# Filler products of ones, a second buffer for the first-stage result and fewer column products in an adaLN, state-space and routed-FFN kernel

## The chip, the cores and the metric

The kernel runs on one core of one Trainium2 chip, in one launch. A core has engines with a queue of instructions each: TensorE (PE in the profile, its weight loads PEld), VectorE (DVE), ScalarE (ACT), GpSimd (POOL) and SyncE (SP, which here only issues transfers). The metric is the device time of one execution in microseconds; before the change three runs took 553.38, 555.62 and 557.21 us, median 555.62.

## The reference, cut to what matters

One sequence of 2048 tokens of width 576 goes through two modulated layers. The shifts, scales and gates are six rows of a product of a condition vector with a 576 x 3456 matrix.

```python
mod = (_silu(c) @ w_mod).reshape(c.shape[0], 6, 1, -1)
sa, ca, ga, sb, cb, gb = (mod[:, i] for i in range(6))
x = A_u
h = _layernorm(x) * (1 + ca) + sa
x = x + ga * _A_ref(h, ...)          # long convolution over the sequence
h = _layernorm(x) * (1 + cb) + sb
x = x + gb * _B_ref(h, ...)          # 8 routed tokens through a SwiGLU FFN
...
def _A_ref(u, ...):                  # D = 576 channels, N = 128 poles, L = 2048
    P = jnp.exp((A * dt[:, None])[:, :, None] * pos[None, None, :])
    K = 2.0 * jnp.einsum("dn,dnl->dl", C, P).real
    y = irfft(rfft(u_t, 2 * L) * rfft(K, 2 * L), 2 * L)[:, :, :L]
    return y + u * D_skip
...
def _B_ref(x, ...):                  # x stays, 8 tokens get an update
    r = x @ w_r
    idx = jnp.argsort(-r, axis=-1)[:, :8]
    y = (_silu(x_sel @ w_gate) * (x_sel @ w_up)) @ w_down   # 576 -> 4608 -> 576
    return x + scatter(y * sigmoid(r_sel))
```

## The kernel before

**Stages.** The long convolution is done as a Fourier transform of length 4096, split in two steps. In the *front* the kernel loads parameters and tokens, makes the modulation rows (`mod_row`, L617 to L650), the layer norm's statistics (`ln_stats`, L681) and the first step of the transform of the tokens (`stage1`, L725): for each of 8 blocks `b` of two token columns, `ln_norm` makes normalised rows `hb` (L720), and four groups of products (L739 for the rows, L742 for the shift) go to two PSUM banks, from where ScalarE or VectorE copies them (L748) to tiles `xs0` and `xs1`. Four transfers of each block (L754) store them to the DRAM tensor `dX`. In the *middle* the convolution reads `dX` back (L912), transforms it (L923), transforms the taps (L937), multiplies, and goes back (L971). The taps come from 36 blocks of poles: magnitudes (L792, L798), sines and cosines (L809 to L832), products (L837 to L858), and a first transform step (L879); some of these blocks are made in the front beside the first stage. In the *tail* the router picks 8 tokens, the FFN weights come in (L1052), and the output is made and stored (L1242 to L1252).

**The order.** Nothing is ordered by a scheduler at run time: `Plan` holds every operation with the engines it may run on, an estimated cost, what it reads and writes, its ring of buffers, and its PSUM banks. `schedule` (L129) puts them in order by a list schedule over those estimates, with priorities from the longest chain to the end, to which seeded noise is added (`SEEDS`, L42); `emit` then writes each engine's queue in the order of planned starts. The planned times are estimates; what runs is the order. Changed costs, buffers or seeds so give a new order for the whole program.

**Rings.** `ring(name, key, bufs)` says that the operations on block `i` of a ring wait in the plan for those on block `i - bufs`; the tile pool gives the tile the same number of buffers. `xs0` and `xs1` have one each: the copies of block `b` wait until the stores of block `b - 1` have ended.

**Fillers.** `spare` (L207) looks at the planned gaps between TensorE's operations. Where a gap holds them, it sets `n` filler products ahead of the later operation, so many that the window of `WINDOW` = 3.4 us before that operation is planned busy to the share `SHARE`, each counted as `UNIT` = 0.27 us. None is set before planned time `FROM` = 12, nor while the bank `b5` is in use by others (from planned time `HOLD` = 130 on, until its last use). `idle` (L433) writes them: a 128 x 128 product of the identity with itself into `b5`, whose result nobody reads.

```python
n = min(int((t1 - t0 - self.GAP) / self.UNIT), math.ceil((self.SHARE * self.WINDOW - full) / self.UNIT))
if n > 0 and (t1 < self.HOLD or t0 > late) and t0 > self.FROM:
```

The identity is part of `csm`, which comes by a transfer (L444). `ones` is a 128 x 1 column that VectorE sets at the start (L429).

**The columns.** Late in the front `cols` (L1394) turns two modulation rows (`cb`, `sb`) into columns, with products of a piece of the row, 64 elements long, with a single one: 2 rows x 5 columns x 2 halves = 20 products (L1401).

A float32 product appears in the trace as two records, a bfloat16 or float16 product as one.

Of the kernel before, what the change touches and what calls it, by code (L numbers as in the profile page):

```python
# [11 lines left out]
F32 = mybir.dt.float32  # L12
# [9 lines left out]
L, D, NS, F = 2048, 576, 128, 4608  # L22
# [15 lines left out]
class Plan:  # L38

    LAT = {"V": .12, "A": .17, "P": .12, "T": .21, "Q": 0.0, "X": 0.0}  # L40
    LOOK, TABLE, RATE, FLY, AHEAD = .3, 1.28, 370.0, 2.0, 2.0
    SEEDS = ((15, 0.32), (789, 1), (1215, 0.32), (1311, 0.32), (1887, 0.32), (3271, 0.32), (4311, 0.32), (5223, 0.32), (5319, 0.32), (13159, 0.32), (16055, 0.32), (23663, 0.32), (35487, 0.32), (35511, 0.32), (36455, 0.32), (37575, 0.32), (39311, 0.32), (43039, 0.32), (62487, 0.32), (94159, 0.32), (220535, 0.32), (314815, 0.32), (322255, 0.32), (349359, 0.32), (362815, 0.32))  # L42
    wide = False
    BANKS, NARROW, HOLD = ("b0", "b1", "b2", "b3", "b4", "b5"), ("b5",), 130.0

# [4 lines left out]
    def ring(self, name, key, bufs):  # L50
        r = self.rings.setdefault(name, [])
        if key not in r:
            r.append(key)
            self.bufs[name, key] = bufs
        return (name, key)
# [73 lines left out]
    def schedule(self):  # L129
        self.link()  # L130
        for s, a in self.SEEDS:
            for o in self.ops:
# [74 lines left out]
    def spare(self):  # L207

        ts = [o for o in self.done if o.on == "T"]
        out, load = {}, []  # L210
        late = max((o.gone for o in self.done if o.need and set(o.names) & set(self.NARROW)), default=0.0)
        for a, b in zip(ts, ts[1:]):
            t0 = a.start + (a.cost["T"] if isinstance(a.cost, dict) else a.cost)
            t1 = b.start
            load.append((a.start, t0))
            while load and load[0][1] < t1 - self.WINDOW:
                load.pop(0)
            full = sum(y - max(x, t1 - self.WINDOW) for x, y in load)
            n = min(int((t1 - t0 - self.GAP) / self.UNIT), math.ceil((self.SHARE * self.WINDOW - full) / self.UNIT))
            if n > 0 and (t1 < self.HOLD or t0 > late) and t0 > self.FROM:  # L220
                out[b] = n
                load.append((t0, t0 + n * self.UNIT))
        return out

    GAP, WINDOW, UNIT, FROM, SHARE, idle = .3, 3.4, .27, 12.0, .8, None

    def emit(self):
        Plan.last = self
# [112 lines left out]
def adaln_s4d_mod_kernel(ctx, tc, u, par0, par1, head, wm, wr, wg, wu, wd, cs, cfg, cmv, out):  # L341
    nc = tc.nc
    V, S, P, T, Q = nc.vector, nc.scalar, nc.gpsimd, nc.tensor, nc.sync
# [11 lines left out]
    def bc(ap, shape):  # L355
        return ap.to_broadcast(shape)
# [29 lines left out]
    su = su_cm.__enter__()  # L386
# [7 lines left out]
    op, ring = plan.op, plan.ring  # L394
# [18 lines left out]
    ident = csm[:, 0:128]  # L413
# [12 lines left out]
    ones = const.tile([128, 1], F32, name="ones")  # L426
# [4 lines left out]
    IDLE = {}  # L431

    def idle(n, late):  # L433

        if "p" not in IDLE or IDLE["late"] != late:
            IDLE["p"], IDLE["late"] = ps.tile([128, 128], F32, name=plan.NARROW[0]), late
        for _ in range(n):
            T.matmul(IDLE["p"], ident, ident, start=True, stop=True)  # L438
    plan.idle = idle
    CH = ((0, 128), (128, D - 128))  # L440
    PP, PAR = {0: pp}, {0: pp.tile([128, 4, 128], F32, name="par0")}
# [162 lines left out]
    for q in range(4):  # L604
        op("AV", {"A": ac(144), "V": vc(144)}, lambda e, q=q: CP[e](
            rdt[32 * q:32 * q + 32].rearrange("p (b x) -> p b x", x=4), gq[32 * q:32 * q + 32, q // 2, q % 2]),
           r=GV, w=[("rdt", q)], tag="su")
    op("V", .95, lambda e: V.reciprocal(rdt, rdt), r=[("rdt", q) for q in range(4)], w=["rdt"], lock=True, tag="su")
    op("V", vc(144), lambda e: stt(dsk2.rearrange("p b x -> p (b x)"), rdt, 0.5, dskr, OP.mult, OP.mult),
       r=["rdt", "hd"], w=["dsk2"], lock=True, tag="su")  # L610
# [41 lines left out]
    def both(w):  # L652
        return [("m", w, 0), ("m", w, 1)]
# [25 lines left out]
    CJ, HB, XS = {}, {}, {}  # L679
# [24 lines left out]
    def ln_rows(j):  # L704
        ring("cj", j, 4)

        def f(e):
            CJ[j] = su.tile([128, 256], F32, name="cj", bufs=4)
            if e == "A":
                S.activation(CJ[j], csm[:, 128:384], AF.Copy, scale=rsn[:, j, 0:1])  # L710
            else:
                ts(CJ[j], csm[:, 128:384], rsn[:, j, 0:1], OP.mult)
        op("V", v2(256), f, r=["csm", ("rs", j)], w=[("cj", j)], lock=True, tag="su")
# [10 lines left out]

    def stage1(b):  # L725
        for m in range(2):
            ring(f"xs{m}", b, 1)
        for j in range(2):
            ln_rows(2 * b + j)
            for hh in range(2):  # L730
                cs_ = slice(288 * hh, 288 * hh + 288)
                st = {}

                def f(e, nm, j=j, cs_=cs_, st=st):
                    st["p"] = pu = banks([128, 288], nm)
                    cj = CJ[2 * b + j].rearrange("p (m o) -> p m o", m=2)
                    for m in range(2):
                        r = slice(64 * m, 64 * m + 64)
                        T.matmul(pu[m], cj[r, m], HB[b][r, j, cs_], start=True, stop=False, tile_position=(64 * m, 0))  # L739
                    for m in range(2):  # L740
                        r = slice(64 * m, 64 * m + 32)
                        T.matmul(pu[m], shc[r], sgs[r, 2, cs_], start=False, stop=True, tile_position=(64 * m, 0))  # L742
                mm = op("T", .75, f, r=["mv", ("hb", b, j), ("cj", 2 * b + j), "sgx"], inst=[("hb", b)], bank=2, tag="su")
                for m in range(2):
                    def g(e, j=j, m=m, cs_=cs_, st=st):
                        if (b, m) not in XS:
                            XS[b, m] = su.tile([128, 2, D], F32, name=f"xs{m}")
                        CP[e](XS[b, m][:, 1 - j if m == 0 else j, cs_], st["p"][m])  # L748
                    op("AV", {"A": ac(288), "V": vc(288)}, g, uses=[mm], w=[("xsp", b, m, j, hh)], inst=[(f"xs{m}", b)],
                       tag="su")  # L750
        for m in range(2):
            s0 = 14 - 2 * b if m == 0 else 2 * b
            for cc in range(2):
                op("Q", .45, lambda e, m=m, cc=cc, s0=s0: Q.dma_start(  # L754
                    dX[cc, m, s0:s0 + 2].rearrange("s h k d -> (h k) s d"), XS[b, m][64 * cc:64 * cc + 64]),
                   r=[("xsp", b, m, j, hh) for j in range(2) for hh in range(2)], inst=[(f"xs{m}", b)],
                   w=[("dX", b, m, cc)], dma=295, tag="su")
# [619 lines left out]
    def swap2(e):  # L1377
# [3 lines left out]
    sb, cb, gb, wrow = ((lambda i=i: m2["p"][:, i]) for i in range(4))  # L1381
# [6 lines left out]
       r=both("cb") + ["wrow"], w=GV + ["vrow", "dtp0", "dtp1"], **lk)  # L1388
# [3 lines left out]
    stc = {}  # L1392

    def cols(e, nm):  # L1394

        stc["p"] = banks([128, 2, 5], nm)[0]
        for i, x in enumerate((cb(), sb())):
            for k in range(5):
                for h in range(2):
                    c = 128 * k + 64 * h if k < 4 else 512  # L1400
                    T.matmul(stc["p"][64 * h:64 * h + 64, i, k:k + 1], x[0:1, c:c + 64], ones[0:1, 0:1],  # L1401
                             start=True, stop=True, tile_position=(0, 64 * h))
    m_ = op("T", 1.2, cols, r=both("cb") + both("sb"), bank=1, tag="su")
    op("AV", {"A": .2, "V": .12}, lambda e: CP[e](csc, stc["p"]), uses=[m_], w=["csc"], tag="su")
    op("V", vc(D), lambda e: tt(ga, gb(), cb(), OP.mult), r=both("gb") + both("cb") + ["cagf", "sagf"], w=both("ga"), **lk)
    op("V", vc(D), lambda e: tt(wrow(), gb(), sb(), OP.mult), r=both("gb") + both("sb"), w=["wrow"], **lk)
# [67 lines left out]
```

## Time and profile before

| what | value |
|---|---|
| median of 3 runs | 555.62 us |
| the profiled execution | 557.26 us, its span 555.5 us |
| mean granted TensorE clock | 0.939 |
| busy: PE, DVE, ACT, POOL | 470.0, 410.5, 322.6, 171.7 us |
| fillers (L438): records, busy on PE | 510, 78.0 us |
| stores `dX<-xs`: count, median to landing | 32, 4.1 us |
| moved by transfers | 96.66 MB, mean 174 GB/s |

The span runs from the first to the last instruction; what lies around it, 1.76 us, is the difference to the execution's own time. Matmuls are pipelined and their ends are modelled, so busy time of PE is not work at its peak. "Granted clock" is the share of TensorE's full clock that the throttle let through. In the chain of waits each piece is the work, transfer or wait that released the next one. Busy times count fillers as work.

### The profile page before, as it was taken

Reading aid. Unit: us, or ns where it says so; the run is one execution under the profiler, and the core shown is the slowest. Engines: PE = TensorE matmul, PEld = TensorE weight load, DVE = VectorE, ACT = ScalarE, POOL = GpSimd, SP = SyncE. Lnnn points to the kernel's source line nnn. Section 1 sums busy time; section 2 is a strip of 40 time slices with the busy share of each in tenths; the row PEclk is TensorE's granted clock in tenths of the full one; section 3 lists DMA queues with packets and bytes.
Section 4 is the critical chain, followed back from the end, with each engine's and each line's share of the span. In section 5 each row is a group of like instructions: output and inputs, shape, how many; then the busy total and the mean of one; then the engine's idle time right before and its main releaser. Section 6 shows DMA issues by size and latency. Waiting matters only on the chain.

```text
span 555.5 us, 17725 instructions
## 1 busy us (share of the span) xinstructions
PE 470.0 (85%) x7589; PEld 330.4 (59%) x7589; DVE 410.5 (74%) x861; ACT 322.6 (58%) x529; POOL 171.7 (31%) x135
## 2 busy tenths in 40 slices
PE   3979898788877789999998899888889479989886
PEld 2755454553556556767676567566778366446453
DVE  4699889877644968798978999979877588554501
ACT  5488579656555879778896897876421003421100
POOL 0003124302212656366836465365722000000000
PEclk9999989887778979999999999999999996999988
DMA  8965333204392211373345323153387899899993
GB/s 349 426 274 173 105 98 88 73 25 128 100 322 90 59 40 61 102 184 100 95 126 146 94 81 99 58 153 117 109 238 200 199 295 383 258 280 379 389 320 144
DMA packets 67285, 96.66 MB, mean 174 GB/s; under 512 B 12891, under 2 KB 46811, under 8 KB 66054
## 3 DMA queue, kind: packets, MB, share of 16 engines
q1 hardware_dynamic: 66070, 92.49, 51.4%
q10 hardware_dynamic: 1104, 3.01, 1.4%
q8 instruction: 60, 0.98, 0.8%
q14 instruction: 19, 0.16, 0.1%
q0 software_dynamic: 32, 0.02, 0.0%
HBM read 71.88 MB, written 23.62 MB: 172 GB/s over the span
## 4 chain that ended last, share of the span: by engine, by line
PE 37%; DVE 22%; DMA 17%; issue 10%; ACT 9%; POOL 3%; SPq 2%; POOLq 0%; DVEq 0%; ACTq 0%
DMA out<-zr 6%; PE b L971 6%; PE b L858 4%; PE b L923 4%; PE b L937 4%; DVE zr L353 4%; DVE n L347 4%; DMA w<-in_wu 3%; PE b L739 3%; PE b L879 3%; DVE Bc L353 3%; DVE t L353 3%; ACT E L798 3%; DMA dX<-xs 2%; DVE E L350 2%
## 5 line engine op out<-in xcount | busy, mean ns | idle before, releaser
L353 POOL TENSOR_TENSOR SC<-SC,E 128x1024 f32<-128x1024 f32 x36 | 87.2, 2424 | 132.4 <-ACT SC L832 61.1
L353 POOL TENSOR_TENSOR t<-t 128x256 f32<-128x256 f32 (+1 forms) x80 | 68.7, 863 | 96.2 <-DVE t L353 94.3
L438 PEld LDWEIGHTS b<-csm 128*128 128x128 f32 x510 | 70.1, 210 | 18.8 <-issue 16.4
L438 PE MATMUL b<-csm 128*128 128x128 f32 x510 | 78.0, 303 | 0.0
L798 ACT ACTIVATE E<-b 128x512 f32<-128x512 f32 x108 | 57.8, 608 | 8.1 <-PE b L792 6.9
L353 DVE TENSOR_TENSOR t<-b,us 128x512 f32<-128x512 f32 (+1 forms) x80 | 47.6, 630 | 12.7 <-PE b L937 10.9
L353 DVE TENSOR_TENSOR Bc<-E,SC 128x1024 f32<-128x1024 f32 x36 | 51.9, 1441 | 0.9 <-PE b L858 0.9
L971 PE MATMUL b<-t,fg 64*128 64x128 f32 (+1 forms) x640 | 45.5, 282 | 5.5 <-POOL t L353 3.3
L828 ACT ACTIVATE SC<-ph 128x1024 f32<-128x1024 f32 x36 | 36.9, 1025 | 21.6 <-PE b L858 7.7
L347 DVE TENSOR_SCALAR n<-ph 128x1024 f16<-128x1024 f32 x36 | 43.8, 1216 | 6.7 <-PE ph L809 6.5
L971 PEld LDWEIGHTS b<-t,fg 64*128 64x128 f32 x640 | 39.0, 187 | 13.6 <-issue 5.9
L923 PE MATMUL b<-xu,fg 128*64 128x128 f32 (+1 forms) x640 | 41.9, 276 | 1.9 <-DVE t L353 0.8
L858 PE MATMUL b<-Bc,SC 128*32 128x64 f32 x1152 | 40.0, 236 | 2.8 <-DVE us L928 0.8
L858 PE MATMUL b<-E,SC 128*32 128x64 f32 x1152 | 39.0, 233 | 3.9 <-DVE E L353 2.2
L832 ACT ACTIVATE SC<-SC,halfpi 128x1024 f32<-128x1024 f32 x36 | 41.3, 1147 | 0.1
L923 PEld LDWEIGHTS b<-xu,fg 128*64 128x64 f32 x640 | 34.3, 142 | 11.5 <-issue 4.8
L1242 ACT ACTIVATE zr<-hx,rs 128x576 f32<-128x576 f32 x16 | 12.8, 861 | 48.8 <-DVE rs L350 31.3
L792 PE MATMUL b<-mv,s 128*128 128x512 f16 x108 | 35.0, 394 | 6.6 <-ACT E L798 4.7
L937 PE MATMUL b<-xk,fg 128*64 128x128 f32 (+1 forms) x640 | 39.6, 270 | 0.7 <-ACT E L798 0.2
L1326 POOL DMA_INDIRECT out<-yo,icol x1 | 1.0, 1041 | 126.2 <-DVE yo L353 126.2
L350 DVE SCALAR_TENSOR_TENSOR E<-E,SC 128x512 f32<-128x512 f32 x36 | 36.7, 1019 | 1.0
L937 PEld LDWEIGHTS b<-xk,fg 128*64 128x64 f32 x640 | 32.6, 139 | 7.5 <-issue 1.9
(231 smaller groups left out, 871.5 us busy)
## 6 DMA issues: line engine op xcount, KB each, us to landing
w<-in_wd SPq DMA_DIRECT2D x12, 864.0 KB, 10.0
dX<-xs SPq DMA_DIRECT2D x32, 288.0 KB, 4.1
w<-in_wg SPq DMA_DIRECT2D x12, 768.0 KB, 5.3
w<-in_wu SPq DMA_DIRECT2D x12, 768.0 KB, 9.5
wt<-in_wm SPq DMA_DIRECT2D x6, 1440.0 KB, 14.7
xu<-dX SPq DMA_DIRECT2D x32, 256.0 KB, 3.1
dZ<-zs SPq DMA_DIRECT2D x32, 256.0 KB, 2.3
zr<-dZ SPq DMA_DIRECT2D x64, 128.0 KB, 3.3
```

The costliest lines, as they stand in the source:

```text
L347: (eng or V).tensor_scalar(o, a, s1, s2, op0=op0, **({"op1": op1} if op1 is not None else {}))
L350: V.scalar_tensor_tensor(o, a, s, b, op0=op0, op1=op1, **kw)
L353: (eng or V).tensor_tensor(o, a, b, op=op)
L438: T.matmul(IDLE["p"], ident, ident, start=True, stop=True)
L792: T.matmul(p, par[b][si], mv[:, i], start=True, stop=True)
L798: S.activation(ES[b][:, h], st["p"], AF.Exp)
L828: S.activation(sc()[:, :, 0], PH[b], AF.Abs)
L832: op("A", ac(1024) + .13, lambda e: S.activation(SCS[b][:, :, 0], SCS[b][:, :, 0], AF.Sin, scale=-TWO_PI, bias=halfpi), w=[("ca", b), ("cb ...
L858: T.matmul(kp[32 * t4:32 * t4 + 32, x], SC[:, 0, ri, 32 * i:32 * i + 32], mo[ri][:, i], start=ri == 0, stop=ri == 1, tile_position=(0, 32 ...
L923: T.matmul(pu[64 * a:64 * a + 64, q, cc], f2[:, 2 * q + a, cc], xu[:, 2 * q + a], start=True, stop=True)
L937: T.matmul(pk[64 * a:64 * a + 64, q, cc], f2[:, 2 * q + a, cc], xk[:, k0 + 2 * q + a], start=True, stop=True)
L971: T.matmul(pz[a][:, q], g2[r, 2 * q + cc], pr[r, q, 1 - cc], start=cc == 0, stop=cc == 1, tile_position=(64 * a, 0))
```

## The change

Four edits. The fillers multiply ones with ones (a broadcast of the column `ones` on both sides) in place of the identity; they may be set from planned time 1.0 on, and also ahead of TensorE's first operation; and the share to which a window is filled is 0.92 in place of 0.80 up to the last use of `b5`, and 0.80 as before after it. `xs0` and `xs1` get two buffers. The planner's cost of a store of the first-stage result on SyncE's queue is 0.8 in place of 0.45. The columns of the first four pieces are made with one product of 128 elements in place of two of 64, so 12 products in place of 20, and the planner's cost is 0.7 in place of 1.2. `SEEDS` is another list, so the order is another.

```diff
-    SEEDS = ((15, 0.32), (789, 1), (1215, 0.32), ...
+    SEEDS = ((5, 1), (55, 0.32), (63, 0.32), ...
...
-        for a, b in zip(ts, ts[1:]):
-            t0 = a.start + (a.cost["T"] if isinstance(a.cost, dict) else a.cost)
+        for a, b in zip([None] + ts, ts):
+            t0 = a.start + (a.cost["T"] if isinstance(a.cost, dict) else a.cost) if a else self.FROM
             t1 = b.start
-            load.append((a.start, t0))
+            if a:
+                load.append((a.start, t0))
...
-            n = min(int((t1 - t0 - self.GAP) / self.UNIT), math.ceil((self.SHARE * self.WINDOW - full) / self.UNIT))
-            if n > 0 and (t1 < self.HOLD or t0 > late) and t0 > self.FROM:
+            share = self.SHARE[t0 > late]
+            n = min(int((t1 - t0 - self.GAP) / self.UNIT), math.ceil((share * self.WINDOW - full) / self.UNIT))
+            if n > 0 and (t1 < self.HOLD or t0 > late):
...
-    GAP, WINDOW, UNIT, FROM, SHARE, idle = .3, 3.4, .27, 12.0, .8, None
+    GAP, WINDOW, UNIT, FROM, SHARE, idle = .3, 3.4, .27, 1.0, (.92, .8), None
...
-            T.matmul(IDLE["p"], ident, ident, start=True, stop=True)
+            T.matmul(IDLE["p"], bc(ones, [128, 128]), bc(ones, [128, 128]), start=True, stop=True)
...
-            ring(f"xs{m}", b, 1)
+            ring(f"xs{m}", b, 2)
...
-                            XS[b, m] = su.tile([128, 2, D], F32, name=f"xs{m}")
+                            XS[b, m] = su.tile([128, 2, D], F32, name=f"xs{m}", bufs=2)
...
-                op("Q", .45, lambda e, m=m, cc=cc, s0=s0: Q.dma_start(
+                op("Q", .8, lambda e, m=m, cc=cc, s0=s0: Q.dma_start(
...
-                for h in range(2):
-                    c = 128 * k + 64 * h if k < 4 else 512
-                    T.matmul(stc["p"][64 * h:64 * h + 64, i, k:k + 1], x[0:1, c:c + 64], ones[0:1, 0:1],
+                for h in range(1 if k < 4 else 2):
+                    c, n = (128 * k, 128) if k < 4 else (512, 64)
+                    T.matmul(stc["p"][64 * h:64 * h + n, i, k:k + 1], x[0:1, c:c + n], ones[0:1, 0:1],
                              start=True, stop=True, tile_position=(0, 64 * h))
-    m_ = op("T", 1.2, cols, r=both("cb") + both("sb"), bank=1, tag="su")
+    m_ = op("T", .7, cols, r=both("cb") + both("sb"), bank=1, tag="su")
```

More of the change, by code (lines that the diff above doesn't have):

```diff
@@ L41 @@
     LOOK, TABLE, RATE, FLY, AHEAD = .3, 1.28, 370.0, 2.0, 2.0
-    SEEDS = ((15, 0.32), (789, 1), (1215, 0.32), (1311, 0.32), (1887, 0.32), (3271, 0.32), (4311, 0.32), (5223, 0.32), (5319, 0.32), (13159, 0.32), (16055, 0.32), (23663, 0.32), (35487, 0.32), (35511, 0.32), (36455, 0.32), (37575, 0.32), (39311, 0.32), (43039, 0.32), (62487, 0.32), (94159, 0.32), (220535, 0.32), (314815, 0.32), (322255, 0.32), (349359, 0.32), (362815, 0.32))
+    SEEDS = ((5, 1), (55, 0.32), (63, 0.32), (189, 1), (279, 0.32), (335, 0.32), (983, 0.32), (4383, 0.32), (5703, 0.32), (18399, 0.32), (32567, 0.32), (35447, 0.32), (46567, 0.32), (156343, 0.32), (162871, 0.32), (272111, 0.32), (281391, 0.32), (282783, 0.32), (332647, 0.32), (384183, 0.32))
     wide = False
```

## The prediction

> **What bounds the kernel now.** I read the page first, for the shares and the clock; then the stretches, to find where the engines stand idle; then the chain of waits over the front; then the order of TensorE's instructions, for the gaps in it. The page:
>
> ```profile
> span 555.5 us, 17725 instructions
> PE 470.0 (85%) x7589; PEld 330.4 (59%) x7589; DVE 410.5 (74%) x861; ACT 322.6 (58%) x529; POOL 171.7 (31%) x135
> PEclk9999989887778979999999999999999996999988
> PE 37%; DVE 22%; DMA 17%; issue 10%; ACT 9%; POOL 3%; SPq 2%; POOLq 0%; DVEq 0%; ACTq 0%
> ```
>
> No single engine fills the span. The clock row is what bears on filler products: it dips in slices 7 to 15 (83 to 208 us) and again late. The same page by stretch (start:end, length, then busy time of PE, PEld, DVE, ACT, POOL, the granted clock, the share of the DMA engines, GB/s):
>
> ```profile
> 8.70:24.30 15.60, 15.20 (x124) 12.11 (x128) 9.33 (x34) 6.66 (x20) 0.00 (x0) 1.00 1.03 432
> 24.30:163.70 139.40, 117.40 (x1427) 73.38 (x1426) 112.19 (x230) 96.04 (x163) 31.97 (x15) 0.89 0.43 140
> ...
> 202.00:426.00 224.00, 202.34 (x4450) 153.72 (x4448) 192.06 (x344) 166.19 (x265) 121.88 (x103) 1.00 0.41 119
> 426.00:555.50 129.50, 104.19 (x965) 68.49 (x963) 67.60 (x197) 20.76 (x32) 1.04 (x1) 0.91 0.88 292
> ...
> 68.00:74.50 6.50, 6.50 (x63) 3.73 (x66) 4.37 (x7) 5.14 (x6) 2.35 (x1) 0.50 0.34 83
> ...
> 130.00:146.50 16.50, 14.57 (x143) 8.40 (x144) 9.20 (x15) 6.31 (x13) 6.70 (x3) 0.59 0.26 74
> ```
>
> The middle (202 to 426) is bound by TensorE and VectorE together, at 90% and 86%, and its clock is whole. The tail (426 on) is bound by transfers, at 0.88. Both follow the front and would move with its end. The change acts in the front, up to 163.7 us, where the first convolution product starts. There VectorE is busy 112.19 of 139.40 us (80%), so there is room, and TensorE stands at half clock in places. The chain of waits over the front (start, length, what):
>
> ```profile
> 8.70 2.79 PE b L626 x40
> 11.49 1.25 PE b L590 x4
> 12.74 2.22 PE b L640 x8
> 14.96 1.26 PE b L590 x4
> 16.21 2.76 PE b L626 x40
> ...
> 19.33 2.29 PE b L640 x8
> 21.61 2.71 PE b L438 x16
> 24.32 1.54 PE b L626 x40
> ...
> 53.36 3.47 DMA dX<-xs
> ...
> 61.84 4.15 DMA dX<-xs
> ...
> 125.71 5.64 DMA dX<-xs
> ...
> 140.29 0.85 PE b L438 x4
> 141.14 2.23 PE b L1401 x40
> ```
>
> Three things on it are what the change touches: an opening in which TensorE runs slowly, three waits of 13.26 us in all for the store of the first-stage result, and the 40 records of the modulation columns. TensorE's instructions in order of time, with the idle time before them in brackets:
>
> ```profile
> 29.71 2.62 PE L438 MATMUL b<-csm 128*128 128x128 f32 x22
> 33.38 0.59 PE L809 MATMUL ph<-mv,s 128*128 128x512 f16 x2 [1.05 <-ACT SC L830]
> ...
> 57.38 0.75 PE L739 MATMUL b<-hb,cj 64*128 64x288 f32 x2 [0.42 <-ACT xs L748]
> 66.54 0.75 PE L739 MATMUL b<-hb,cj 64*128 64x288 f32 x2 [0.95 <-ACT xs L748]
> ...
> 82.97 1.25 PE L640 MATMUL b<-sm,csm 128*128 128x144 f32 x8
> ...
> 98.93 1.01 PE L819 MATMUL ph<-n,mv 128*128 128x512 f16 x2 [3.34 <-DVE n L347]
> 131.99 0.75 PE L739 MATMUL b<-hb,cj 64*128 64x288 f32 x2 [1.93 <-DVE xs L748]
> ```
>
> One float32 product is two records, so a filler takes 2 x 2.62/22 = 0.24 us. The clock, not the work, explains the opening: the group at L640 takes 2.29 us at 19.33 and 1.25 us at 82.97. The clock row shows 1.00 for 8.70 to 24.30 all the same; there I believe the durations.
>
> **The opening.** Filler products read the identity now, which comes by a transfer, and none is set before planned time 12. The ones are set by VectorE at the very start:
>
> ```profile
> 0.84 0.06 DVE L429 MEMSET ones<- 128x1 f32 x1
> ...
> 20.69 0.46 DVE L649 COPY mod<-b 128x288 f32<-128x288 f32 x1 [1.88 <-PE b L640]
> ...
> 24.89 0.81 DVE L685 BATCH_NORM_STATS2 bs<-hx 128x6 f32<-128x288 f32 x2
> ```
>
> So up to ceil(0.92 x 3.4/0.27) = 12 products can run from about 0.9 us. At half clock one takes 0.24 x 2.29/1.25 = 0.44 us, the twelve 5.3 us; they end near 6.2 and leave 2.5 us of idle before the first weights at 8.70. (Longer by 2.5 us, they would hold up the product there.) A gap of 1.93 us (at 131.99) was enough to bring the half clock, one of 1.05 (at 33.38) was not. So I expect the products at 8.70 to start cold still, and to be brought up by the next run of fillers, as the 16 records at 21.61 did it here within their 2.71 us. The excess on the chain is 1.25 and 1.22 (L626 against 1.54, the same group at 24.32), 0.97 and 1.04 (L640 against 1.25), and half of 1.25 and 1.26 (L590, no warm row): 5.7 us at most, nothing at least. Waiting behind it is VectorE's queue, as the 1.88 us at 20.69 shows; what is late next is the token input, for the statistics at 24.89. I take half: 2.8 us.
>
> The Trainium skill, TensorE: Matmul & The Clock Gate, Part 1 and the table of why this matters, says that about 3.4 us of sustained matmuls release the half clock and that gaps below about 3 us do not bring it back. By that the opening would be warm at 8.70 and the whole 5.7 us would go; but by it the 12.6 us of unbroken work from 8.70 would also have released the clock, and the trace shows that they did not, and that 1.93 us sufficed to lose it.
>
> **Two buffers for the first-stage result.** The copies at L748 then wait for the store of two blocks earlier. What they wait now, over both engines, and the filler products of the front:
>
> ```profile
>   DMA dX<-xs: 9.0, 8
> ...
> L438 PE MATMUL b<-csm x202: 270/275/582, 21.4 to 151.0; 128*128 128x128 f32 x101
> ```
>
> The 13.26 us of the chain is no gain by itself, since the engines have other work in the meantime. The bounds are 0 and 9.0 us; nearest to the end of the kernel is what TensorE lost, 0.42 + 0.95 + 1.93 = 3.3 us, which I take. Next late are the copies themselves behind the products, and VectorE. No step is moved to another queue; the 32 stores stay SyncE's, and the planner's 0.8 in place of 0.45 for each changes only the order. The second pair of tiles costs no instruction.
>
> **The clock after those waits.** From 130 to 146.5 the clock is 0.59, and where it is low throughout, as from 68 to 74.5, it is 0.50: (1 - 0.59) x 2 x 16.5 = 13.5 us at half speed, on the chain nearly throughout, so 6.8 us lost. It begins with the 1.93 us gap that the buffer takes away. The bounds are 0 and 6.8; I take half, 3.4, because another gap may stand in its place. From 68 to 74.5 the clock is 0.50: 3.25 us lost, behind the 0.95 us gap; half is 1.6. The cold pieces behind the 3.34 us gap at 98.93 have VectorE as their cause and I leave them.
>
> **Twelve products for the columns.** 40 records take 2.23 us, 0.056 each; 24 are left, so 0.9 us goes, on the chain (between 0, if VectorE's end decides instead, and 1.1, half of it).
>
> **The denser fillers.** Raising the share from 0.80 to 0.92 of 3.4 us allows 0.41 us more, 1.5 products, in each 3.4 us: over the 127 us from 24.3 to 151 at most 56 more, beside 101 now. They are set in gaps of the plan; where the plan's gap is not real, they stand ahead of work. Of today's 202 records 42 lie on the chain, in six pieces from 21.61 to 140.29, 7.72 us together, 0.37 us a product. The same share of 56 is 11.6 products, 4.3 us lost (2.8 at 0.24 each, 5.1 at 0.44; 0 if every new gap is real). That a product of ones takes as long as one of the identity I assume: no row has a broadcast moving operand on TensorE, and the stationary one, L640, is not slow.
>
> **The order.** New seeds plan the whole program anew. No row prices it; as an estimate, a fifth of the 21.7 us that TensorE idles in the middle (224.00 - 202.34), 4 us either way, and 0 in the sum.
>
> **The sum.** 2.8 + 3.3 + 3.4 + 1.6 + 0.9 - 4.3 = 7.7 us. VectorE allows it: without the opening's 2.8, 112.19 us of work in 139.4 - 4.9 = 134.5 us is 83%, below the 86% it holds in the middle. The profiled execution took 557.26 us (555.5 of span and 1.76 around it), so 549.6; it lay 1.64 us above the median 555.62, so against the median 547.9: **548 us**, and 543 to 553 for this case with the order's 4 us and the halves.
>
> **The rivals.** (1) The clock stays whole in the front, as the page's rule would have it with fillers this dense. Then 5.7 + 3.3 + 6.8 + 3.25 + 0.9 - 2.8 = 17.2 us goes, 538.5 us; VectorE would need 112.19/127.9 = 88%. For it: the fillers at 21.61 did bring the clock up. Against it: the gap at 98.93 is VectorE's, and products cover only planned gaps. (2) The gains stay in the front: VectorE or ScalarE becomes late where the store was, the half clock finds another gap, and only the columns' 0.9 us shows, 555 us. For it: 9.0 us of waits spread over eight places are small against VectorE's 80%. Against it: from 130 to 146.5 TensorE, not VectorE (9.20 of 16.5), sets the pace. (3) Slower: with two buffers the first-stage products (L739) are bunched, and one more gap of over 1 us in front of such a bunch brings a second stretch like that of 132 to 146, in which 13 us of these products did not bring the clock back. It costs 6.8 us, none of the clock gains come, and 0.9 is saved: 557.26 + 5.9 - 1.64 = 561.5 us. It decides from the point at which two such stretches stand before 164 us.
>
> **How the numbers follow.** Chances: forecast 0.47, whole clock 0.17, no gain 0.24, slower 0.12. A measurement of this kernel tells about 1% from no change: 550.1 to 561.2. Of the forecast 0.33 falls below 550.1 and 0.14 above; with rival (1) faster is 0.50, with rival (2) the same is 0.38, and slower is 0.12. The range reaches from 539, leaving out half of rival (1), to 560, leaving out most of rival (3).
>
> **What would show it.** The groups L626 and L640 before 24 us: at 1.6 and 1.25 us the opening is warm, at 2.8 and 2.3 nothing was won. ScalarE's and VectorE's waits at the copies for the store: near 0 if the buffer does what it says. The clock between 60 and 150 us, and whether a stretch like 132 to 146 is there. The column group: 24 records, some 1.3 us. Filler pieces on the chain: 12 us in place of 7.7 by my term. The first convolution product: about 156 in place of 163.7; if it comes at 156 and the total does not follow, the middle's order ate it. Wrong I am if the middle, from the first convolution product to 426, changes its length by over 4 us.

## The result, and the profile after

The changed kernel took 540.46 us in the median of four runs (538.86 to 543.23), the kernel before beside it 556.41. The ratio is 0.971, 95% interval 0.963 to 0.979: faster. The profiled execution took 538.90 us, its span 537.1. (The ratios leave out runs more than 1.5% above the fastest of the same kernel on the same chip, the medians do not; the kernel before has up to four such runs in seven, so the two can differ by one per cent.)

The forecast was 548 us, 543 to 553 for the likeliest case, with a range from 539 to 560. The direction and the wide range held, the narrower one did not; the gain is twice the size of the forecast. Part of it came from where I had put nothing, the order.

The page of the changed kernel, the rows that answer to those of before:

```profile
span 537.1 us, 17733 instructions
PEclk7989989999989999989999999999999777899899
PE 37%; DVE 24%; DMA 15%; ACT 11%; issue 9%; SPq 3%; POOL 0%; POOLq 0%; ACTq 0%; DVEq 0%
```

The clock row now shows the opening at half clock (slice 1: 7), which the row of before did not. It dips between 34 and 42 us and between 70 and 84 us, is whole from 84 to 153 us, and has lost the dips of before (69 to 83 us and 97 to 208 us) but for small ones. Busy time by stretch (start:end, length, then PE, PEld, DVE, ACT, POOL, the granted clock, share of the DMA engines, GB/s):

```profile
68.00:74.50 6.50, 3.66 (x32) 2.94 (x25) 6.47 (x11) 6.45 (x8) 2.80 (x2) 1.00 0.37 121
72.00:82.00 10.00, 5.29 (x82) 4.36 (x81) 9.83 (x23) 3.95 (x5) 3.71 (x2) 0.67 0.01 2
100.00:140.00 40.00, 38.97 (x423) 20.87 (x417) 31.67 (x65) 27.99 (x56) 4.33 (x3) 1.00 0.76 217
130.00:146.50 16.50, 13.62 (x283) 9.36 (x279) 10.32 (x18) 12.87 (x24) 4.68 (x2) 1.00 0.86 254
```

The stretch at half clock from 130 to 146.5 is gone (0.59 before, 1.00 now). The first-stage products, spread over 45 to 147 us before, stand mostly together from 100 to 133 us, at full clock. In the groups of records of TensorE, the first and the last start of the convolution's transform and of its inverse mark the ends of the front and of the middle:

```profile
L925 PE MATMUL b<-xu,fg x640: 222/272/476, 154.6 to 405.2; 128*64 128x128 f32 x128, 128*64 128x64 f32 x32
...
L973 PE MATMUL b<-t,fg x640: 230/272/373, 163.9 to 409.9; 64*128 64x128 f32 x128, 64*128 64x64 f32 x32
```

and of the kernel before:

```profile
L923 PE MATMUL b<-xu,fg x640: 222/273/476, 163.7 to 422.8; 128*64 128x128 f32 x128, 128*64 128x64 f32 x32
...
L971 PE MATMUL b<-t,fg x640: 272/272/373, 183.0 to 427.4; 64*128 64x128 f32 x128, 64*128 64x64 f32 x32
```

Of the 18.4 us of the two spans (555.5 and 537.1), the front gave 9.1 (163.7 to 154.6), the middle 8.4 (263.7 us long before, 255.3 now) and the tail 0.9. I had 7.7 us, all of it in the front, and the middle unchanged. These are two single executions, that of before 0.85 us above its median and that of after 1.56 us below; a second profile of the changed kernel, with a span of 538.9 us, has 157.4, 255.1 and 126.4 us for front, middle and tail, where the first has 154.6, 255.3 and 127.2.

### The profile page after: what moved, and what is told of

Its sections match the earlier page's. It is cut to its first block, busy times and chain, and to the rows that moved or that the text cites. A ratio compares the mean times of both kernels' runs of the same rounds, so it can differ in the third digit from the quotient of the medians.

```text
span 537.1 us, 17733 instructions
## 1 busy us (share of the span) xinstructions
PE 460.8 (86%) x7593; PEld 327.7 (61%) x7593; DVE 414.9 (77%) x867; ACT 316.2 (59%) x523; POOL 167.8 (31%) x133
## 4 chain that ended last, share of the span: by engine, by line
PE 37%; DVE 24%; DMA 15%; ACT 11%; issue 9%; SPq 3%; POOL 0%; POOLq 0%; ACTq 0%; DVEq 0%
PE b L860 5%; PE b L973 5%; DMA out<-zr 5%; PE b L939 4%; DVE Bc L355 4%; DVE n L349 4%; PE b L925 3%; PE b L741 3%; DVE t L355 3%; DVE zr L355 3%; PE b L881 3%; DVE E L352 3%; PE b L794 2%; ACT E L800 2%; DMA w<-in_wu 2%
## 5 line engine op out<-in xcount | busy, mean ns | idle before, releaser
L355 POOL TENSOR_TENSOR t<-t 128x256 f32<-128x256 f32 (+1 forms) x80 | 67.3, 849 | 86.9 <-DVE t L355 85.1
L440 PEld LDWEIGHTS b<-ones 128*128 128x128 f32 x530 | 74.9, 213 | 20.6 <-issue 17.1
L440 PE MATMUL b<-ones 128*128 128x128 f32 x530 | 83.6, 306 | 1.0 <-DVE ones L431 1.0
L355 DVE TENSOR_TENSOR Bc<-E,SC 128x1024 f32<-128x1024 f32 x36 | 54.9, 1526 | 5.5 <-PE b L860 4.6
L830 ACT ACTIVATE SC<-ph 128x1024 f32<-128x1024 f32 x36 | 36.9, 1025 | 24.9 <-PE b L860 11.1
L860 PE MATMUL b<-Bc,SC 128*32 128x64 f32 x1152 | 38.1, 227 | 8.2 <-issue 6.8
L925 PE MATMUL b<-xu,fg 128*64 128x128 f32 (+1 forms) x640 | 40.7, 271 | 3.9 <-ACT E L800 2.3
L925 PEld LDWEIGHTS b<-xu,fg 128*64 128x64 f32 x640 | 32.7, 139 | 12.8 <-ACT E L800 3.6
L860 PE MATMUL b<-E,SC 128*32 128x64 f32 x1152 | 36.9, 225 | 3.9 <-DVE E L355 3.9
L860 PEld LDWEIGHTS b<-Bc,SC 128*32 128x32 f32 x1152 | 27.5, 113 | 17.2 <-issue 14.6
L832 ACT ACTIVATE SC<-ph 128x1024 f32<-128x1024 f32 x36 | 36.7, 1020 | 0.2
```

Of the source, the lines that this page charges most:

```text
L355: (eng or V).tensor_tensor(o, a, b, op=op)
L440: T.matmul(IDLE["p"], bc(ones, [128, 128]), bc(ones, [128, 128]), start=True, stop=True)
L830: S.activation(sc()[:, :, 0], PH[b], AF.Abs)
L832: op("A", ac(1024), lambda e: S.activation(sc()[:, :, 1], PH[b], AF.Sin, scale=TWO_PI), r=[("ph", b)], w=[("sa", b), ("sb", b)], inst=[("S ...
L860: T.matmul(kp[32 * t4:32 * t4 + 32, x], SC[:, 0, ri, 32 * i:32 * i + 32], mo[ri][:, i], start=ri == 0, stop=ri == 1, tile_position=(0, 32 ...
L925: T.matmul(pu[64 * a:64 * a + 64, q, cc], f2[:, 2 * q + a, cc], xu[:, 2 * q + a], start=True, stop=True)
```

## The experiments

The parts were taken apart with the order of the instructions held fast: after the plan is made, buffers, fillers and columns can be changed where the instructions are written, and every queue keeps its order. Two theories stood against each other: that the edits themselves carry the gain (parts), and that the new order of the whole program does (order).

**The buffer alone, in the old order.**

```diff
-                            XS[b, m] = su.tile([128, 2, D], F32, name=f"xs{m}")
+                            XS[b, m] = su.tile([128, 2, D], F32, name=f"xs{m}", bufs=2)
```

> The kernel before with two buffers for the first-stage tiles and nothing else: the plan still holds one, so every queue has the order of before. Parts theory (the gain is that of the edits themselves): the copies' 9.0 us of waits for the stores go, the gap of 1.93 us at 132 us goes, and with it the stretch at half clock from 132 to 146; the first convolution product comes at 155 to 160 in place of 163.7 and the time is 546 to 551 us. Order theory (the gain is that of the new order of the whole program): the waits go, but the front ends where it did, within 2 us, and the time is 553 to 557 us.

Measured: 543.10 us against 553.73, ratio 0.991 (0.983 to 0.999); by the median more than either theory had. The same kernel again, and beside it on the same chip the changed kernel again, both as they were:

> The kernel before with two buffers and nothing else, in the order of before, once more beside the changed kernel. Wait theory (the second buffer carries most of the gain): 541 to 545 us, 0 to 4 us above the changed kernel. If new order and fillers carry more than a third: 546 us or more.

> The changed kernel itself once more, on the chip of the three runs beside it, since its first time came from another chip than the experiments. If the chip makes no difference: 539 to 543 us, and 8 to 14 us under the median of the kernel before.

Measured: 545.97 us for the buffer and 540.89 for the changed kernel, against 555.46; ratios 0.987 (0.982 to 0.992) and 0.977 (0.972 to 0.982). So the buffer alone gives 9.5 us of 14.6 by the medians, two thirds, and 1.3 of 2.3 per cent by the ratios, a little over half. The copies of the first-stage result in this run:

```profile
its engine sat idle before it (us, times) until:
  PE b L742: 11.9, 22
```

No wait for a store is left (9.0 us before), and what was late next is the products themselves, 11.9 us where it was 14.2 with the stores. The front ends at 150.4 us, 13.3 earlier than before, and the middle is nearly as long as it was (261.2):

```profile
L923 PE MATMUL b<-xu,fg x640: 222/273/476, 150.4 to 407.0; 128*64 128x128 f32 x128, 128*64 128x64 f32 x32
...
L971 PE MATMUL b<-t,fg x640: 272/272/373, 168.0 to 411.6; 64*128 64x128 f32 x128, 64*128 64x64 f32 x32
```

The second run lies 5.1 us over the changed kernel, a little outside what the wait theory had said (0 to 4). So the rest of the gain is probably not the buffer's; the two intervals just touch, and in the first run the buffer alone had 543.10.

**Is it the wait, or the half clock behind it?** Here the wait stays, but TensorE is given work in it.

```diff
+                    CALLS.append(b)
                     for m in range(2):
+                        if m and len(CALLS) == 27:
+                            idle(8, False)
```

> The kernel before, with one buffer and its own order and fillers, and 8 more products of the identity (16 records, 1.9 us at full clock) between the two halves of the 27th first-stage group, where TensorE stood idle for 1.93 us at 130 us while the copy waited for a store. The wait itself stays. Clock theory (the wait costs little by itself; the half clock that follows it costs most): no stretch at half clock after 132 us, first convolution product at 156 to 158 us, 546 to 550 us. Wait theory (the engines' time in the wait is what counts): the time stays within 2 us of the kernel before, 552 to 557 us.

Measured: 549.93 us against 551.15, ratio 1.0005 (0.997 to 1.004): no difference. TensorE in order of time, with idle time in brackets:

```profile
128.84 2.05 PE L438 MATMUL b<-csm 128*128 128x128 f32 x16
...
133.20 0.76 PE L743 MATMUL b<-hb,cj 64*128 64x288 f32 x4
...
136.86 1.33 PE L1405 MATMUL b<-ones,m 1*64 1x1 f32 x40 [0.48 <-ACT s L783]
140.76 1.01 PE L823 MATMUL ph<-n,mv 128*128 128x512 f16 x2 [2.57 <-DVE n L347]
143.57 1.33 PE L743 MATMUL b<-hb,cj 64*128 64x288 f32 x4
```

The mechanism is there: with the gap filled, the first-stage products behind it run at full clock (0.76 us for four records, where the kernel before took 1.33 for the same from 133 us on), until the next gap of 2.57 us, which follows the 40 column products; there they are slow again. The first convolution product comes at 158.9, 4.8 us earlier than in the profile of before. The time does not show it. The median lies in the range of the clock theory, but the kernel before beside it lies at 551.15, so what was won is what the wait theory said, nothing. That does not settle it, because the copies waited longer for the stores than before (11.6 us in place of 9.0) and less than half of the cold time went. The copies' waits in this run, and the stretch from 24 to 150 us before, with the gap filled, and with two buffers (the second run):

```profile
  DMA dX<-xs: 11.6, 10
```

```profile
24.00:150.00 126.00, 109.07 (x1214) 67.51 (x1214) 104.16 (x214) 87.31 (x149) 28.71 (x14) 0.89 0.38 124
...
24.00:150.00 126.00, 107.84 (x1236) 68.02 (x1225) 108.00 (x215) 89.23 (x150) 29.42 (x14) 0.92 0.39 128
...
24.00:150.00 126.00, 104.53 (x1414) 66.66 (x1406) 113.37 (x230) 95.31 (x163) 31.62 (x15) 0.97 0.47 152
```

In these profiles the second buffer takes away the waits and most of the half clock at once (granted clock 0.89 before, 0.96 and 0.97 with it). How its gain divides between the two stays open. Why 4.8 us in one profiled execution are not 4.8 us in the medians is open too; only one execution of the kernel before was profiled.

**The fillers alone, and all three edits, in the old order.** The first takes over `spare` and the products of ones, the second also the buffer and the 12 column products. The edits of the first, in the kernel before:

```diff
-        for a, b in zip(ts, ts[1:]):
+        for a, b in zip([None] + ts, ts):
...
-            n = min(int((t1 - t0 - self.GAP) / self.UNIT), math.ceil((self.SHARE * self.WINDOW - full) / self.UNIT))
-            if n > 0 and (t1 < self.HOLD or t0 > late) and t0 > self.FROM:
+            share = self.SHARE[t0 > late]
+            n = min(int((t1 - t0 - self.GAP) / self.UNIT), math.ceil((share * self.WINDOW - full) / self.UNIT))
+            if n > 0 and (t1 < self.HOLD or t0 > late):
...
-            T.matmul(IDLE["p"], ident, ident, start=True, stop=True)
+            T.matmul(IDLE["p"], bc(ones, [128, 128]), bc(ones, [128, 128]), start=True, stop=True)
```

> The kernel before with the new fillers alone (ones, from planned time 1, share 0.92 in the front), every other instruction in the order of before. Parts theory: the opening is warm by about 14 us and shorter by 3 to 5 us, the stretch at half clock from 132 to 146 stays, 550 to 554 us. Order theory: 554 to 557 us. If denser fillers stand in the way, as the prediction's term of 4.3 us has it, 556 to 560 us.

Measured: 553.12 us against 553.73, ratio 1.007 (0.999 to 1.016): nothing won, and nothing lost that could be told.

And what the second adds to them:

```diff
-                            XS[b, m] = su.tile([128, 2, D], F32, name=f"xs{m}")
+                            XS[b, m] = su.tile([128, 2, D], F32, name=f"xs{m}", bufs=2)
...
-                for h in range(2):
-                    c = 128 * k + 64 * h if k < 4 else 512
+                for h in range(1 if k < 4 else 2):
+                    c, n = (128 * k, 128) if k < 4 else (512, 64)
```

> The kernel before with all three edits (buffers, fillers, 12 column products) and the order of before: what is left to the changed kernel is the order alone. Parts theory: 540 to 546 us, near the changed kernel's 540.5. Order theory: 551 to 556 us, and the changed kernel is faster by 10 us or more at equal parts.

Measured: 543.01 us against 553.73, ratio 0.992 (0.984 to 1.000), the same as the buffer alone on the same chip (543.10). In the old order nothing beyond the buffer's gain can be told, though an interval of 1.6% leaves room for some us.

**The new order without the new fillers.**

```diff
-        for a, b in zip([None] + ts, ts):
+        for a, b in zip(ts, ts[1:]):
...
-    GAP, WINDOW, UNIT, FROM, SHARE, idle = .3, 3.4, .27, 1.0, (.92, .8), None
+    GAP, WINDOW, UNIT, FROM, SHARE, idle = .3, 3.4, .27, 12.0, .8, None
...
-            T.matmul(IDLE["p"], bc(ones, [128, 128]), bc(ones, [128, 128]), start=True, stop=True)
+            T.matmul(IDLE["p"], ident, ident, start=True, stop=True)
```

> The changed kernel with the fillers of before (the identity, none before planned time 12 nor ahead of the first operation, share 0.80) and every other instruction in its order. If the fillers matter (parts theory): the opening runs at half clock to 20 us or more, other stretches at half clock appear between 30 and 150 us, 545 to 550 us. If they do not: 540 to 542 us.

Measured: 548.37 us against 553.73 (541.45 to 556.11 in four runs), ratio 0.993 (0.978 to 1.008): too wide to place by itself. Its profiled execution, one of the two longer ones (550.03 us), began the convolution at 164.2 us, seven to ten later than the changed kernel, though its middle was as short (256.2). Whether the new order is worth anything without the new fillers is therefore open.

**The new order without the opening products.**

```diff
-            if n > 0 and (t1 < self.HOLD or t0 > late):
+            if n > 0 and a and (t1 < self.HOLD or t0 > late):
```

> The changed kernel without the 12 products ahead of TensorE's first operation, all other fillers kept. If they warm the opening (parts theory): the groups of the modulation rows run at half clock until 18 us or later, and the time is 2 to 3 us more, 542.5 to 544 us. If the 3.95 us gap behind them undoes it: the same opening as in the changed kernel, 540 to 541 us.

Measured: 543.82 us (551.15 for the kernel before beside it), ratio 0.990 (0.985 to 0.995); the changed kernel 540.5 and 540.9 on other chips. The opening of this kernel:

```profile
8.95 2.29 PE L592 MATMUL b<-dx,ones 64*128 64x144 f32 x8 [8.95 <-DVE dx L355]
...
11.89 2.79 PE L628 MATMUL b<-wt,scb 128*32 128x144 f32 x40
15.07 2.29 PE L642 MATMUL b<-sm,csm 128*128 128x144 f32 x8 [0.40 <-ACT sm L635]
...
17.72 2.73 PE L628 MATMUL b<-wt,scb 128*32 128x144 f32 x40
...
22.31 1.57 PE L628 MATMUL b<-wt,scb 128*32 128x144 f32 x40
```

and of the changed kernel:

```profile
0.96 4.28 PE L440 MATMUL b<-ones 128*128 128x128 f32 x24 [0.96 <-DVE ones L431]
9.19 2.29 PE L592 MATMUL b<-dx,ones 64*128 64x144 f32 x8 [3.95 <-DVE dx L355]
...
12.13 2.47 PE L628 MATMUL b<-wt,scb 128*32 128x144 f32 x40
15.00 1.25 PE L642 MATMUL b<-sm,csm 128*128 128x144 f32 x8 [0.40 <-ACT sm L635]
...
19.92 1.57 PE L628 MATMUL b<-wt,scb 128*32 128x144 f32 x40
```

In both the work from 9 us on starts at half clock; the twelve opening products, which end at 5.2 us, are followed by 3.95 us of idle. But the clock comes back before 15.0 instead of before 20.9, and the third row's products start at 19.92 instead of 22.31: 2.4 us in these two traces. The medians differ by 2.9 to 3.4 us, across chips; a kernel with the opening products on this chip (the one with 20 columns, below) took 541.06 us, ratio 0.984 (0.979 to 0.989), and the intervals overlap, so the time alone does not prove it.

In the new order the third row starts at 19.9 to 20.5 us in all four profiles with the twelve products, and at 21.7 and 22.3 in the two without. In the old order it is less sure: with the same twelve products it starts at 22.33 in one run (the fillers alone) and in the other (all three edits) as late as without them (23.6 to 24.3 in four runs):

```profile
24.71 1.57 PE L628 MATMUL b<-wt,scb 128*32 128x144 f32 x40
```

**A longer opening, and the 20 columns.** 28 products instead of 12, so that the gap closes; and, alone and with it, the 20 column products of before.

```diff
+            n = n if a else 28
             if n > 0 and (t1 < self.HOLD or t0 > late):
```

> The changed kernel with 28 products ahead of TensorE's first operation in place of 12, and with the 20 column products of before. The opening products then end near 9 us instead of 5.2, where the first real product starts. If the 3.95 us gap is what leaves the first products cold: the group at 9.2 us takes 1.2 in place of 2.29 us, the first group of the modulation rows 1.57 in place of 2.47, 2.0 us go there and up to 1.1 in the columns, 537 to 540 us. If they hold up the first product or the front waits for the transfers anyway: 540 to 543 us.

Measured: 540.47 us beside 540.89 of the changed kernel, ratio 0.976 (0.970 to 0.981) to the kernel before: no difference to the changed kernel that could be told. The opening did become warm:

```profile
0.96 8.34 PE L441 MATMUL b<-ones 128*128 128x128 f32 x56 [0.96 <-DVE ones L432]
9.23 1.24 PE L593 MATMUL b<-dx,ones 64*128 64x144 f32 x8
10.70 1.57 PE L629 MATMUL b<-wt,scb 128*32 128x144 f32 x40 [0.22 <-DVE vrow L596]
13.66 1.25 PE L643 MATMUL b<-sm,csm 128*128 128x144 f32 x8 [1.40 <-ACT sm L636]
```

but its next product now waits 1.40 us for a copy on ScalarE, where it waited 0.40: past the changed kernel's opening, the copy on ScalarE is late there, not TensorE.

The 20 columns alone, in the changed kernel:

```diff
-                for h in range(1 if k < 4 else 2):
-                    c, n = (128 * k, 128) if k < 4 else (512, 64)
+                for h in range(2):
+                    c = 128 * k + 64 * h if k < 4 else 512
```

> The changed kernel with the 20 column products of before, in the same order of the queues. In the changed kernel the 24 records took 2.44 us at full clock, in the kernel before with the new fillers the 40 records took 1.33 us at full clock. If the time of this group is on the way to the end: 1.1 us less than the changed kernel, 539 to 540 us. If it is hidden: no difference.

Measured: 541.06 us, ratio 0.984 (0.979 to 0.989) on its chip; the changed kernel 540.5 and 540.9 elsewhere. No gain can be told, but the interval is wider than the 1.1 us in question: whether the group's time is hidden stays open. The chain of the changed kernel does have the group on it, with 2.37 us. The edit itself made the group slower. Of the changed kernel:

```profile
135.08 2.44 PE L1403 MATMUL b<-ones,m 1*128 1x1 f32 x24
```

and of this run, at the same full clock:

```profile
135.07 1.33 PE L1403 MATMUL b<-ones,m 1*64 1x1 f32 x40
```

**Ones or the identity.** The changed kernel with the identity in all fillers but the twelve of the opening.

```diff
-                self.idle(fill[o], o.start > self.HOLD)
+                self.idle(fill[o], o.start > self.HOLD, o.start > 10)
...
-            T.matmul(IDLE["p"], bc(ones, [128, 128]), bc(ones, [128, 128]), start=True, stop=True)
+            x = ident if eye else bc(ones, [128, 128])
+            T.matmul(IDLE["p"], x, x, start=True, stop=True)
```

> The changed kernel with products of the identity in place of ones after planned time 10; the 12 opening products stay ones. If only the moment at which the operand is there matters: the same time as the changed kernel within 1 us, and the same clock. If products of ones hold the clock better: lower clock between 30 and 120 us and 2 us or more on top.

Measured: 543.10 us, ratio 0.980 (0.975 to 0.985), beside 0.977 (0.972 to 0.982) of the changed kernel. The intervals overlap; whether ones are worth the 2.2 us between the medians is open. Up to 22 us the two run alike.

**The old seeds with the new plan.** The changed kernel with the list of seeds of before: all edits, but a third order.

```diff
-    SEEDS = ((5, 1), (55, 0.32), (63, 0.32), (189, 1), (279, 0.32),
...
+    SEEDS = ((15, 0.32), (789, 1), (1215, 0.32), (1311, 0.32), (1887, 0.32),
...
```

> The changed kernel with the seeds of before: all edits, planned anew, another order than both. If the seeds carry the order's part: 545 to 552 us. If any order planned with two buffers will do: 540 to 544 us.

Measured: 570.72 us against 551.15, ratio 1.040 (1.033 to 1.047), far outside both ranges. The order alone makes 30 us against the changed kernel here. Of the two spans, 567.5 and 537.1 us, 8.9 us of the difference stand in the front, 10.9 in the middle and 10.6 in the tail:

```profile
L925 PE MATMUL b<-xu,fg x640: 216/273/476, 163.5 to 423.5; 128*64 128x128 f32 x128, 128*64 128x64 f32 x32
...
L973 PE MATMUL b<-t,fg x640: 272/272/579, 195.3 to 429.7; 64*128 64x128 f32 x128, 64*128 64x64 f32 x32
```

Stretches of its front:

```profile
100.00:110.00 10.00, 10.00 (x82) 4.41 (x84) 6.25 (x14) 5.23 (x8) 0.50 (x1) 0.50 0.68 188
...
140.00:150.00 10.00, 10.00 (x40) 3.63 (x36) 3.38 (x9) 3.17 (x9) 0.00 (x0) 0.50 0.38 108
```

and TensorE behind the gap that began the first, and ahead of the second:

```profile
90.72 0.44 PE L860 MATMUL b<-Bc,SC 128*32 128x64 f32 x8 [7.30 <-ACT m L649]
...
92.58 1.33 PE L741 MATMUL b<-hb,cj 64*128 64x288 f32 x4
...
135.28 2.55 PE L1403 MATMUL b<-ones,m 1*128 1x1 f32 x24
137.76 1.33 PE L741 MATMUL b<-hb,cj 64*128 64x288 f32 x4
```

The picture of rival (3) of the prediction is here, in another order: the first-stage products bunched (all between 92.6 and 149.7 us) and two whole stretches of 10 us, TensorE busy throughout, at clock 0.50. Only the first has a gap in front; ahead of the second stand the column products. But the two stretches do not account for the time: the front ends at 163.5 us, where it ended before (163.7), and what this kernel loses against the kernel before is in the middle (2.5 us) and the tail (9.7 us).

## Why the prediction was right, and where it was wrong

**The order was the step that failed.** I put 0 in the sum, 4 us either way, and wrote that I would be wrong if the middle changed its length by over 4 us. It changed by 8.4 in the two profiles. Over all profiled kernels the middle, from the first transform's product to the last of the inverse, is 260.7 to 266.5 us long in the six executions with the old order (mean 263.0) and 255.1 to 258.0 in the seven with the new (mean 256.4), whatever the buffers and fillers: 6.6 us are the order's. Rows of the middle, before, with the buffer alone, with all three edits in the old order, and changed:

```profile
163.70:427.40 263.70, 234.61 (x5112) 177.75 (x5108) 218.05 (x380) 193.39 (x308) 138.49 (x115) 0.97 0.39 115
```

```profile
150.40:411.60 261.20, 234.05 (x5110) 176.56 (x5108) 218.66 (x380) 193.34 (x308) 138.92 (x115) 0.98 0.40 117
```

```profile
154.40:418.00 263.60, 232.58 (x5116) 176.19 (x5108) 219.36 (x380) 193.51 (x309) 138.70 (x115) 0.99 0.40 118
```

```profile
154.60:409.90 255.30, 230.75 (x4981) 173.33 (x4982) 220.82 (x374) 190.65 (x302) 134.84 (x113) 0.99 0.38 111
```

TensorE has some 130 records less to do in the new middle and 3.3 us less of busy time against the buffer alone, and it idles 24.6 us in place of 27.2. The missing records are those of the taps' first step (L879, L881 after): 128 of them stood ahead of the first convolution product before, 256 now. The new order so moves work from the middle into the front. Its front is 154.6 and 157.4 us long in the changed kernel, 154.4 with all three edits in the old order, and 150.4 and 151.5 with the buffer alone. The net is smaller than 6.6 us and not sharply known: at equal parts the medians differ by 2.1 to 2.6 us, across chips, and beside the buffer alone on one chip by 5.1 us, in which fillers and columns are contained. That the total came to lie within 539 to 560 us is in part luck: the order's share, which I had at 0, and a gain of the front larger than my terms. The price of an order cannot be read from the idle time of one profile, as I tried: with the old seeds it was 30 us the other way.

**Two buffers: the mechanism right, the split open.** I took what TensorE idled, 3.3 us, within 0 to 9.0. With the two clock terms behind it (3.4 and 1.6) that is 8.3 us; the buffer alone measured 9.5 to 10.6 by the medians and 4.8 to 7.2 by the ratios (0.9 and 1.3 per cent). The sum is of the right size. How it divides is not shown: filling the gap, without taking the wait away, won nothing that could be told, so the waits of the copies themselves, the upper bound of 9.0, may have been the better price. They stand in the in-order queues of ScalarE and VectorE, where what stands behind them waits too, not TensorE alone; but filling the gap also left longer waits and most of the half clock. In the changed kernel 3.0 us of these waits are back:

```profile
  DMA dX<-xs: 3.0, 5
```

because the new order puts the blocks close together. No gap of TensorE over 0.5 us comes of it, though one wait for a store, 4.13 us at 125.59, is still on the chain, where there were three of 13.26 us.

**The opening: right in the new order.** 2.8 us were forecast; in the new order the twelve products bring some 2 us in the traces, and the time does not contradict it. In the old order one of two runs had nothing of it. That the work at 9 us would start cold behind the gap was right as well. Closing the gap brings nothing more that could be told; ScalarE is next there.

The gaps bear on the Trainium skill's rule (TensorE: Matmul & The Clock Gate, the table of why this matters: no idle gaps above about 3 us). Behind a gap of 1.93 us in the kernel before, and one of 3.95 us in the changed one, the products ran at half clock, so here less than the page's 3 us sufficed. Part 1 of the same page of the Trainium skill has about 3.4 us of sustained matmuls release it; the two stretches of 10.00 us busy at 0.50 above speak against that for first-stage products, while the fillers did release it.

But I had read a threshold between 1.05 and 1.93 us out of one profile, and the length of a gap alone does not decide. In the old order TensorE has a gap of 1.8 us at the same place in every run. Behind it the next ten records of fillers ran mostly cold before, and warm with two buffers:

```profile
114.32 0.38 PE L792 MATMUL b<-mv,s 128*128 128x512 f16 x1 [1.81 <-ACT E L798]
...
117.28 2.19 PE L438 MATMUL b<-csm 128*128 128x128 f32 x10
```

```profile
109.06 0.38 PE L792 MATMUL b<-mv,s 128*128 128x512 f16 x1 [1.83 <-ACT E L798]
...
111.25 1.38 PE L438 MATMUL b<-csm 128*128 128x128 f32 x10
```

The clock fell behind this gap in four of the six runs with the old order and stayed whole in the two with the buffer alone. So a stretch at half clock in one profile need not stand in another run, and my clock terms rested on one profile. The unbroken work from 8.70 us that I named also has an idle time of 0.40 us in it, and of the stretch from 132 to 146 us only the first seven us are mostly first-stage products.

**The denser fillers: wrong.** I had 56 more in the front and 4.3 us of harm. The changed kernel has 108 products there in place of 101, the twelve of the opening among them:

```profile
L440 PE MATMUL b<-ones x216: 270/273/581, 1.0 to 138.9; 128*128 128x128 f32 x108
```

The share was not what limited them, but the gaps of the plan: without the twelve, the new rule sets 103 products in the old order where the old rule set 101. On the chain they are five pieces and 4.50 us, where they were six and 7.72; in the second profile of the changed kernel they are nine and 6.65 us. In the old order the new fillers changed the time by nothing that could be told. That a product of ones takes as long as one of the identity held: 273 and 275 ns a record in the median.

**The columns: wrong in sign.** I had 0.9 us saved by counting records. The 24 records take 2.44 us where 40 take 1.33 at the same clock. What that does to the time is too small to be told.

**The rivals.** The number came out nearest to rival (1), 538.5 us, and not by its mechanism: the front's clock is not whole. It falls in the opening, between 34 and 42 us, and behind a gap that VectorE leaves at 73 to 78 us, as I had argued against it. What rival (3) describes, bunched first-stage products at half clock, stands in the trace of the kernel with the old seeds, but not in the order that the change chose; and the 570.7 us of that kernel are not its work alone, since its front ends no later than before.

## What to carry to other kernels

Where an in-order queue waits for a buffer, the idle time of another engine can be too low a price for the wait: a second buffer for the first-stage tiles was worth 5 to 10 us where TensorE had idled 3.3 and the copies had waited 9.0. A change that plans the order anew cannot be priced from the edit; its parts can be tried with the order held fast, and the order be judged by how long the same stage is over several runs. Fewer products are not less time where they were running side by side. A stretch at half clock that stands in one profile may be missing in the next run, so a term built on it needs a second profile.

## What the runs showed of the hardware that was not expected

Products with one moving column cost by their spacing, not by their number: 24 records, 16 of them with 128 stationary columns, came 0.10 us apart (2.44/24), 40 records with 64 columns, alternating between the two halves of the array, 0.033 us apart (1.33/40), though each took 0.19 us (192 ns). The Trainium skill (TensorE: Matmul & The Clock Gate, Part 3) has products in separate column groups overlap; the trace agrees, and the edit gave that up for most of them. A weight load of 128 columns also took longer than one of 64 (186 and 133 ns); no run separates the two.

TensorE can lose its clock without standing idle. In the second profile of the changed kernel the 24 column records, 2.44 us of them from 134.5 us on, had no idle time before or behind them that the trace shows, and the products from 137.6 us on ran at half clock; with the old seeds, where no gap before them was longer than 0.5 us, the same came behind 2.55 us of them. In the first profile of the changed kernel the clock stayed whole.

First-stage products, each with 64 rows of the array, kept the full clock for 30 us when they came to it warm (100 to 133 us in the changed kernel, with a few other products between them) and did not win it back in 16 and 13 us when they came cold (92.6 to 108.7 and 137.8 to 150.6 us with the old seeds, granted clock 0.50), with TensorE busy nearly throughout in all three. What the throttle counts, that these products hold it and do not raise it, no run here says.
